# First x tiles first on the ACT ring, fold copies by PSUM bank, last tile in column halves, a new order table

## The chip, the cores and the metric

The kernel runs on one core of a Trainium2 chip. The metric is the device time of one execution in microseconds; 264.27 us is the median of four runs of the kernel before (263.08 to 264.51).

A core has five engines that run their own instruction queues in order: TensorE (PE in the profile, with its weight loads as PEld), VectorE (DVE), ScalarE (ACT), GpSimd (POOL) and SyncE (SP), which here only issues DMAs. ScalarE issues a few DMAs too. [...]

## The reference

One block with adaptive normalisation. x is [1, 2048, 448], c is [1, 448]. Six rows of modulation come from c; then a linear attention with a softmax feature map, then a gated MLP that mixes over the sequence:

```
sa, ca, ga, sb, cb, gb = silu(c) @ w_mod
h = layernorm(x) * (1 + ca) + sa
q, k, v = h @ wqkv                               # 16 heads of 28
phi(p) = concat(softmax(p @ w_phi), softmax(-p @ w_phi))
kv = phi(k)^T v ; z = sum over s of phi(k)
x = x + ga * ((phi(q) kv) / (phi(q) z + 1e-6)) @ wo
h = layernorm(x) * (1 + cb) + sb
z1, z2 = split(gelu(h @ w_in))                   # 896 columns each
g = w_sp @ layernorm(z2) + b_sp                  # w_sp is 2048 x 2048
x = x + gb * (z1 * g) @ w_out
```

All inputs and the output are bf16.

## The kernel before

The program has a fast path, and a general path behind a branch that is taken only when a bound on the exponents fails. All of the profile is the fast path. It works on 16 tiles of 128 rows of x; x stays in SBUF from the start to the end (f_x), and so do the weights. Four stages follow each other, and overlap:

* **The head**, to about 12 us. The loads are issued, x tiles 0 and 1 are normalised and transposed by TensorE (turn_mm, turn_out), the columns 1 + ca and sa are made from c and w_mod (columns, 16 tiny matmuls for each), and w_phi and 1 + ca are folded into the key weights: wk is transposed (fold_T), copied out of PSUM (L742), multiplied with a block diagonal BD of w_phi (fold_pf), and scaled (fold_W). Row 448 of the folded weights carries the bias from sa (fold_sa and the copy after it). keep_busy issues matmuls whose result nobody reads.
* **Keys and values**, to about 57 us. For each tile i: k.i and v.i are four matmuls each, e.i.0 and e.i.1 the exponentials of +p and -p, rd, rc and mu the sum, the reciprocal and the product that make the softmax, vc the copy of v, and kv eight matmuls that accumulate kv over all tiles. In between, the query weights are folded (fq, sq, pq), the second norm's columns are made (cfb), the gates (gt), and queries are projected (qp, and q for single pieces) with their exponentials (qpe, qe). gs, gr and grc square the folded weights and sum them for the bound. bn, ag, rp, la1, ld1 and lT normalise x tiles 2 to 15 and transpose them, mostly by a DMA (lT) that SP issues; tm and to do it with TensorE.
* **Outputs of the attention and the MLP's first half**, to about 137 us. For each tile: num (eight matmuls), sx, cr, dn, ri, w and t (the division and the product), ad on GpSimd, oT (a transposing DMA), wo, xc (the residual), ls, la, rs and ap (the second norm), h2T (a transposing DMA), z2 and its gelu ge, zs, za and zn (the norm of z2). z1.st.fc with its gelu zg makes z1 for four tiles at a time. ws scales the MLP's weights by 1 + cb, wg the output weights by ga.
* **The gated product**, from 137 us: for each of four column blocks of w_sp and each of seven feature blocks 16 matmuls (g_unit), then VectorE adds and multiplies, and the output tiles (o_mm, o_fin) follow one block behind.

What each engine does in which order is written by hand. The head stands as straight code; from there a string ORDER lists words like `k.3` or `e.3.0`, and a loop calls the step of each word in turn. Every step puts its instructions at the ends of its engines' queues, so the string fixes the order of each queue. `ld.n` are loads on SP's queue: 3 is x tiles 12 to 15, 4 the second 960 columns of modulation (840 KB), 7 and 9 the gates' weights, 5 and 6 the halves of w_in, 8 wo. `wsp.0.u` is one of eight transposing loads of the first w_sp block. ca and cc are memsets and small copies on GpSimd.

PSUM tiles of one bank come from four buffers (bank, bank_bf), those of two banks from two (bank2). A step that takes a buffer waits for the last reader of its former tile; most waits of TensorE on ScalarE are of this kind.

SP's and ACT's DMAs share eight completion semaphores in turn, so each DMA also waits for the one eight places ahead of it.

Of the kernel before, what the change touches and what calls it, by code (L numbers as in the profile page):

```python
# [15 lines left out]
P = 128  # L16
D = 448
# [5 lines left out]
FC = 7  # L23
# [455 lines left out]
CB = HP * DH  # L479
# [39 lines left out]


def fast_path(tc, A_x, A_wqkv, A_w_phi, A_wo, B_w_in, B_w_sp, B_b_sp, B_w_out, c, w_mod, out, flag):
# [182 lines left out]
    def l1_ag(i):  # L704
        nc.vector.bn_aggr(out=l1_pair(i), in_=l1bn.pop(i)[:])
# [7 lines left out]
    def l1_rstd(q):  # L713
        l1rs[q] = rstd_of(l1mv.pop(q), 2, "l1", RD if 2 * q in BY_ACT else -1.0)
# [67 lines left out]
    for i in range(2):  # L782
# [39 lines left out]


    Eq = eqp.tile([P, 4, 2, S], BF, name="f_Eq")
# [440 lines left out]
    nc.scalar.copy(out=ot[:, 0:D // 2], in_=last[3][:, 0:D // 2])  # L1265
    nc.scalar.dma_start(out=outv[15][:, 0:D // 2], in_=ot[:, 0:D // 2])
    nc.vector.tensor_copy(out=ot[:, D // 2:D], in_=last[3][:, D // 2:D])
# [53 lines left out]
```

## Time and profile before

| what | value |
|---|---|
| median of the runs | 264.27 us |
| profiled execution | 263.18 us |
| its span | 261.4 us |
| granted clock of TensorE | 0.994 |
| busy: PE, PEld | 248.6, 128.7 us |
| busy: DVE, ACT, POOL | 162.6, 107.8, 90.3 us |
| share of PE in the chain that ended last | 83% |
| first statistics of x (VectorE) | 5.42 us |
| first exponential of k (ScalarE) | 16.53 us |
| first num (TensorE) | 56.31 us |
| first g matmul (TensorE) | 137.28 us |

The span runs from the first to the last instruction; the execution's own time is a little longer. A matmul's end is modelled: two that follow each other overlap in the record, and the distance between starts is what one costs (four k matmuls start within 0.76 us, though they are recorded as 0.92 busy). L and a number is a line of the kernel. "issue" in the chain is time in which the engine waited for nothing that the profile shows, SPq and ACTq are the engines' queues.

### The profile page before, as it was taken

The page shows a single profiled execution, that of the slowest core. Times are in us where ns is not written, and L with a number is a line of the kernel's source. Part 1 is how long each engine was busy: PE and PEld are TensorE (multiplying, and loading weights), DVE is VectorE, ACT ScalarE, POOL GpSimd, SP SyncE. Part 2 cuts the span into 40 slices and gives each one's busy share as a digit, 9 for nine tenths or more (in the row PEclk, how much of TensorE's full clock was granted, in tenths as well). Part 3 has the DMA queues.
Part 4 walks back from the last instruction along what each step waited for, and adds up shares of the span by engine and source line. Part 5 has one row for each costly group of instructions (what it writes and reads, how often), then busy time and mean ns, then how long its engine had stood idle before and what let it go on. Part 6 is the DMA issues. An engine that isn't in the chain of part 4 may idle for free.

```text
span 261.4 us, 4412 instructions
## 1 busy us (share of the span) xinstructions
PE 248.6 (95%) x1570; PEld 128.7 (49%) x1590; DVE 162.6 (62%) x364; ACT 107.8 (41%) x208; POOL 90.3 (35%) x201
## 2 busy tenths in 40 slices
PE   6789999999998999999999999999999999999991
PEld 3555666675554555444444444444444444444450
DVE  3889989999999989968062454342533434342540
ACT  2499777979775478887986000000000000000000
POOL 5787871004888778766340092000000000000000
PEclk9999999999999999999999999999999999999997
DMA  7975889605666334144499999951000000001002
GB/s 179 294 208 100 158 174 127 214 3 42 136 119 89 63 61 63 31 91 82 83 189 191 245 185 173 171 117 36 18 0 18 20 30 5 0 20 35 19 20 63
DMA packets 69057, 25.29 MB, mean 97 GB/s; under 512 B 59105, under 2 KB 68898, under 8 KB 69026
## 3 DMA queue, kind: packets, MB, share of 16 engines
q1 hardware_dynamic: 68066, 24.12, 48.0%
q10 hardware_dynamic: 960, 0.80, 1.2%
q8 instruction: 14, 0.23, 0.4%
q14 instruction: 17, 0.14, 0.2%
HBM read 8.92 MB, written 1.84 MB: 41 GB/s over the span
## 4 chain that ended last, share of the span: by engine, by line
PE 83%; DVE 5%; DMA 4%; ACT 3%; issue 2%; POOL 1%; ACTq 0%
PE g_ps L1213 37%; PE z_ps L832 17%; PE o_ps L1220 8%; PE v_ps L832 4%; PE k_ps L832 4%; PE x_ps L1105 3%; PE kvacc L866 3%; DMA f_wm<-in_w_mod_dram 2%; PE q_ps L832 2%; DVE t L1074 2%; DMA oT<-f_opad 2%; PE num L1045 2%; PE b_ps L778 1%; ACT f_Wsq L955 1%; ACT f_E L839 0%
## 5 line engine op out<-in xcount | busy, mean ns | idle before, releaser
L1213 PE MATMUL g_ps<-f_wsp,f_z2n 128*128 128x512 bf16 x328 | 73.7, 379 | 0.4
L1213 PEld LDWEIGHTS <-f_z2n 128*128 128x128 bf16 x448 | 43.7, 98 | 52.0
L1215 DVE TENSOR_TENSOR gb<-g_ps,f_bsp 128x512 f32<-128x512 f32 x28 | 19.4, 692 | 68.1 <-PE g_ps L1213 63.6
L1265 ACT CAST ot<-o_ps 128x224 bf16<-128x224 f32 x1 | 0.3, 345 | 114.6 <-PE o_ps L1220 114.6
L832 PE MATMUL z_ps<-f_win,h2T 128*128 128x448 bf16 (+1 forms) x128 | 26.9, 352 | 0.5 <-DMA h2T<-f_xpad 0.4
L1128 DVE BATCH_NORM_STATS2 z2st<-z2g 128x6 f32<-128x448 bf16 x32 | 19.2, 614 | 11.7 <-ACT z2g L1167 11.6
L832 PE MATMUL z_ps<-h2T,f_win 128*128 128x512 bf16 (+1 forms) x107 | 26.0, 379 | 0.3
L1080 POOL TENSOR_TENSOR f_opad<-t 128x448 bf16<-128x448 bf16 x16 | 16.8, 1056 | 23.5 <-DVE t L1074 22.9
L1213 PE MATMUL g_ps<-f_hT,f_z2n 128*128 128x512 bf16 x109 | 24.7, 379 | 0.2
L1220 PE MATMUL o_ps<-f_wout,f_z1T 128*128 128x448 bf16 x112 | 23.5, 352 | 0.0
L1216 DVE TENSOR_TENSOR f_z1T<-gb,f_z1T 128x512 bf16<-128x512 f32 x28 | 20.1, 716 | 1.0
L1178 ACT ACTIVATE f_z1T<-z_ps,f_b 128x512 bf16<-128x512 f32 x28 | 18.2, 683 | 3.7 <-PE z_ps L832 3.7
L832 PEld LDWEIGHTS <-h2T 128*128 128x128 bf16 (+1 forms) x128 | 12.0, 97 | 12.0 <-DMA h2T<-f_xpad 1.0
L850 DVE TENSOR_REDUCE ksum<-f_E 128x32 f32<-128x896 bf16 x16 | 16.9, 1074 | 1.7 <-ACT f_E L839 1.5
L1171 ACT ACTIVATE f_z2n<-z2g,nm,rs 128x896 bf16<-128x896 bf16 x16 | 17.8, 1128 | 0.3 <-POOL nm L1142 0.3
L1167 ACT ACTIVATE z2g<-z_ps 128x896 bf16<-128x896 f32 x16 | 14.6, 918 | 6.7 <-PE z_ps L832 5.3
L832 PEld LDWEIGHTS <-f_win 128*128 128x128 bf16 x112 | 10.9, 97 | 12.8
L1074 DVE TENSOR_TENSOR t<-num,w 128x896 bf16<-128x896 f32 x16 | 17.0, 1085 | 0.1
L839 ACT ACTIVATE f_E<-k_ps 128x448 bf16<-128x448 f32 x32 | 16.1, 561 | 1.8 <-issue 1.1
L1220 PEld LDWEIGHTS <-f_z1T 128*128 128x128 bf16 x112 | 10.9, 98 | 10.9
L832 PEld LDWEIGHTS <-f_hT 128*128 128x128 bf16 (+1 forms) x128 | 11.5, 97 | 8.7 <-issue 0.5
L832 PE MATMUL v_ps<-f_Wv,f_hT 128*128 128x448 bf16 x64 | 14.6, 352 | 0.4 <-ACT junk L968 0.4
(148 smaller groups left out, 337.3 us busy)
## 6 DMA issues: line engine op xcount, KB each, us to landing
out_dram<-ot SPq DMA_DIRECT2D x15, 112.0 KB, 1.7
f_x<-in_A_x_dram SPq DMA_DIRECT2D x3, 448.0 KB, 6.9
f_win<-in_B_w_in_dram SPq DMA_DIRECT2D x2, 672.0 KB, 5.3
f_wm<-in_w_mod_dram SPq DMA_DIRECT2D x1, 840.0 KB, 6.8
f_wout<-in_B_w_out_dram SPq DMA_DIRECT2D x1, 784.0 KB, 5.2
f_bsp<-in_B_b_sp_dram SPq DMA_DIRECT2D x1, 512.0 KB, 5.1
f_wm<-in_w_mod_dram ACTq DMA_DIRECT2D x1, 448.0 KB, 6.3
f_wm<-in_w_mod_dram SPq DMA_DIRECT2D x1, 392.0 KB, 6.8
```

The costliest lines, as they stand in the source:

```text
L832: nc.tensor.matmul(out, lhsT=lhs(kc, last[kc]), rhs=rhs(kc, last[kc]), start=(kc == 0), stop=(kc == KC - 1))
L839: nc.scalar.activation(out=Ering[i % NR][:, s, :], in_=ps["k", i][:, 0:D], func=ACT.Exp, scale=1.0 - 2.0 * s)
L850: nc.vector.tensor_reduce(out=cs["s", i][:], in_=Ering[i % NR][:].rearrange("p s (c f h) -> p (s c) h f", c=4, h=HP), axis=AX.X, op=ALU.add)
L1074: nc.vector.tensor_tensor(out=ts[i][:, 0:2 * D].rearrange("p (s h d) -> p s h d", s=2, h=H), in0=nv(i)[:, :, :, 0:DH], in1=cs.pop(("w", i) ...
L1080: nc.gpsimd.tensor_tensor(out=opad[i % NO][:, 0:D], in0=t[:, 0:D], in1=t[:, D:2 * D], op=ALU.add)
L1128: nc.vector.bn_stats(out=cs["z", i][:, hf, :], in_=z2gs[i][:, hf * D:(hf + 1) * D])
L1171: nc.scalar.activation(out=z2n[:, i, :], in_=z2gs.pop(i)[:], func=ACT.Identity, scale=rstd[:, 1:2], bias=nmr[:, 1:2])
L1178: nc.scalar.activation(out=z1T[:, fc, st * 512:(st + 1) * 512], in_=ps.pop(("z1", st, fc)), func=ACT.Gelu_apprx_tanh, bias=b1[:, fc:fc + 1])
L1213: nc.tensor.matmul(g[:], lhsT=z2n[:, s_, fc * P:(fc + 1) * P], rhs=wsp_tiles[tcn][:, s_, :], start=(s_ == 0), stop=(s_ == NT - 1))
L1215: nc.vector.tensor_tensor(out=gb[:], in0=g[:], in1=bsp[:, tsl], op=ALU.add)
L1216: nc.vector.tensor_tensor(out=z1T[:, fc, tsl], in0=gb[:], in1=z1T[:, fc, tsl], op=ALU.mult)
L1220: nc.tensor.matmul(o_ps, lhsT=z1T[:, fc, t * P:(t + 1) * P], rhs=wout_s[:, fc, :], start=(first and fc == 0), stop=(fc == FC - 1))
```

## The change

Six things differ.

1. The load of wk's last 64 rows goes from ACT's queue to SP's, so that x tiles 0 and 1 stand first on ACT's.
2. The four copies after fold_T are given to ScalarE and VectorE by PSUM bank (g // 2) and no longer in turn (g % 2).
3. rstd of the first tiles stands before BD on GpSimd.
4. The transposes of tile 1 stand before the fold on TensorE, one keep_busy after it, and the copy of that tile goes from VectorE to ScalarE. Statistics of tile 3 stand before the order table.
5. The last output tile is made in two halves of 224 columns, each in a bank of its own, with its own copy and its own DMA.
6. ORDER is a new string with the same words except bn.3 and ag.3 (now ahead of it).

```diff
-    nc.scalar.dma_start(out=wk_raw[0:64, 3, 0:D], in_=A_wqkv[3 * P:D, D:2 * D])
-    nc.sync.dma_start(out=wk_raw[:, 0:3, 0:D], in_=A_wqkv[0:3 * P, D:2 * D].rearrange("(k p) n -> p k n", p=P))
+    load_rows(nc.sync, wk_raw[:, :, 0:D], A_wqkv[:, D:2 * D])
     nc.scalar.dma_start(out=x_sb[:, 0:2, :], in_=xv[:, 0:2, :])
...
-            (nc.vector.tensor_copy if g % 2 else nc.scalar.copy)(out=wT[:, g, 0:D], in_=tps[g // 2][0:CB, g % 2, 0:D])
+            (nc.vector.tensor_copy if g // 2 else nc.scalar.copy)(out=wT[:, g, 0:D], in_=tps[g // 2][0:CB, g % 2, 0:D])
...
+    l1_rstd(0)
     nc.gpsimd.tensor_tensor(out=BD[:].rearrange("p g (f h) -> p g f h", h=HP),
...
-    l1_rstd(0)
     more_constants()
...
     turn_out(0, hT[:, :, 0:P], True)
-    keep_busy(1, 256)
+    turn_mm(1)
     pf01 = bank2("pf01")
...
-    turn_mm(1)
+    keep_busy(1, 256)
     sa_ps = bank("sa_ps")
     fold_sa(wk_raw, sa_ps)
+    turn_out(1, hT[:, :, P:2 * P], True)
     nc.scalar.copy(out=wTk[:, :, D], in_=sa_ps[0:CB, 0:4])
     fold_pf(wTk, 3)
-    turn_out(1, hT[:, :, P:2 * P], False)
+    for i in (2, 3):
+        l1_bn(i)
+        l1_ag(i)
     fold_W(Wk, 3, True)
-    l1_bn(2)
-    l1_ag(2)
...
-    last = [bank2("o_ps")[:, 0, 0:D] if n < 2 else bank("o_ps")[:, 0:D] for n in range(4)]
+    last = [bank2("o_ps")[:, 0, 0:D] if n < 2 else bank("o_ps")[:, 0:D if n == 2 else D // 2] for n in range(5)]
...
-    nc.tensor.matmul(last[3], lhsT=ident[:], rhs=x_sb[:, 15, :], start=True, stop=False)
-    o_mm(last[3], 15, 0, 7, first=False)
     ot = wk.tile([P, D], BF, tag="ot", bufs=4)
-    nc.scalar.copy(out=ot[:, 0:D // 2], in_=last[3][:, 0:D // 2])
-    nc.scalar.dma_start(out=outv[15][:, 0:D // 2], in_=ot[:, 0:D // 2])
-    nc.vector.tensor_copy(out=ot[:, D // 2:D], in_=last[3][:, D // 2:D])
-    nc.sync.dma_start(out=outv[15][:, D // 2:D], in_=ot[:, D // 2:D])
+    for n, (eng, copy) in enumerate(((nc.scalar, nc.scalar.copy), (nc.sync, nc.vector.tensor_copy))):
+        cols = slice(n * D // 2, (n + 1) * D // 2)
+        o_ps = last[3 + n]
+        nc.tensor.matmul(o_ps, lhsT=ident[:], rhs=x_sb[:, 15, cols], start=True, stop=False)
+        for fc in range(FC):
+            nc.tensor.matmul(o_ps, lhsT=z1T[:, fc, 15 * P:16 * P], rhs=wout_s[:, fc, cols], start=False, stop=(fc == FC - 1))
+        copy(out=ot[:, cols], in_=o_ps)
+        eng.dma_start(out=outv[15][:, cols], in_=ot[:, cols])
```

Of the order table, the start, the place where the attention's outputs begin, and the end:

```diff
-cc gs.0 k.0 bv bn.3 wv.2 ag.3 wv.1 bn.4 rp.1 gr.0 bn.5 bvc k.1 ld.7 wv.0 ag.4 wv.3 ag.5 ld.3 bn.7 grc.0 sq rp.2 e.0.0 bn.6 v.0 e.1.0 ld1.3 sqc ag.7
-e.1.1 ld1.2 tm.3 ag.6 bn.10 e.0.1 fq.0 la1.5 vc.0 to.3 fq.1 ag.10 rd.0 la1.4 fqc.2 lT.5 tm.2 k.3 fqc.0 rp.3 fqc.1 to.2 gt.0 rc.0 lT.4 fqc.3 bn.8 e.3.0
...
+ca wv.3 rp.1 k.1 bv wv.0 wv.2 wv.1 bn.4 k.0 bvc bn.5 e.1.1 cc ag.4 ld.4 ld1.2 e.1.0 sq ag.5 bn.7 e.0.0 v.0 ld1.3 sqc ld.7 e.0.1 ag.7 bn.6 tm.2 tm.3
+vc.0 v.1 rp.2 to.2 gs.0 rd.0 k.2 to.3 v.2 rc.0 la1.5 bn.8 vc.1 v.3 bn.10 la1.4 vc.2 ag.6 e.2.0 fq.1 mu.0 rp.3 lT.4 e.2.1 fq.0 bn.9 vc.3 kv.0 ag.8 rd.1
...
-vc.14 zb mu.15 vc.15 wg.2 gs.1 wg.0 kv.14 wg.1 wg.3 kv.15 wb.3 kb1 wb.2 wbc.3 kb2 gr.1 wbc.2 ws.1 num.0 zbc num.1 ws.3 sx.0 q.5 sx.1 cr.0 cr.1 dn.0
...
+rc.15 kv.13 mu.15 v.15 wg.1 wg.2 kv.14 wg.0 vc.15 wb.3 qpe.1.0 kv.15 wb.2 qpe.1.1 kb2 kb1 zb wbc.3 wg.3 gr.1 ws.2 num.0 num.1 ws.1 sx.0 q.7 zbc sx.1
...
-z2.14 zg.2.2 zg.2.3 wsp.0.4 zg.2.4 z1.3.4 ge.13 z1.3.5 wsp.0.7 ge.14 z1.3.6 zs.14.0 z2.15 zg.3.6 zs.14.1 zg.3.4 za.14 zs.13.0 rs.17 z1.3.1 ge.15
-zs.13.1 z1.3.3 za.13 zg.3.1 rs.16 zs.15.0 z1.3.2 zs.15.1 zg.3.3 zn.14 z1.3.0 za.15 rs.18 zg.3.2 zn.13 zn.15 zg.3.5 zg.3.0
...
+z2.14 wsp.0.5 z1.3.6 ge.14 z1.3.3 wsp.0.2 zg.3.6 zs.14.0 zn.12 z2.15 zs.14.1 wsp.0.0 za.14 zs.13.1 zg.3.3 rs.17 z1.3.1 za.13 ge.15 z1.3.5 rs.16 zg.3.1
+zs.15.0 z1.3.0 zs.15.1 zg.3.5 z1.3.4 za.15 zg.3.0 rs.18 zn.14 z1.3.2 zn.13 zn.15 zg.2.6 zg.3.2 zg.3.4
```

Other moves in the table: ld.4 from the place after e.4.1 to the start, ahead of ld.7; ld.3 from the start to the place after gtc.0; q.11 from the attention's outputs to the keys and values; wsp.0.2 and wsp.0.5 from the attention's outputs to the end, wsp.0.4 and wsp.0.7 from the end to the keys and values; ws.2 takes the place of ws.3 ahead of the first product.

## The prediction

> **What bounds the kernel now.** I read the engines by stage first, since a mean over the span mixes stages with different limits. The table of windows gives, by stage, length, then busy time of PE, PEld, DVE, ACT and POOL:
>
> ```profile
> 0.00:12.00 12.00, 8.38 (x108) 5.63 (x109) 6.55 (x22) 4.08 (x9) 7.99 (x51) 1.00 0.90 232
> 12.00:18.00 6.00, 5.05 (x56) 2.71 (x55) 4.87 (x17) 5.69 (x13) 4.27 (x11) 1.00 0.94 261
> 18.00:57.00 39.00, 38.84 (x396) 25.16 (x398) 37.19 (x73) 31.97 (x66) 17.70 (x32) 1.00 0.69 133
> 57.00:86.00 29.00, 27.43 (x196) 15.14 (x195) 28.47 (x82) 20.61 (x55) 19.86 (x32) 1.00 0.56 88
> 86.00:137.00 51.00, 50.73 (x275) 25.24 (x278) 37.34 (x99) 40.89 (x61) 31.88 (x70) 1.00 0.46 83
> 137.00:256.00 119.00, 118.14 (x554) 54.85 (x562) 47.82 (x73) 4.43 (x7) 8.64 (x9) 1.00 0.39 74
> ```
>
> From 18 to 57 and from 86 to 256 us TensorE never rests, so the matmuls themselves set the end there. Time can only come from three places: before 18 us, the 57 to 86 us stage where VectorE is the busier engine (28.5 of 29.0), and the tail. Next the chain that ended last (start, length, what), at the head and the tail:
>
> ```profile
> 1.95 6.26 DMA f_wm<-in_w_mod_dram
> ...
> 12.77 1.31 ACT f_Wsq L955
> 14.08 0.47 ACT f_Wsq L956
> 14.55 0.56 ACT f_Wv L878
> ...
> 16.63 0.87 ACT f_E L839 x2
> 17.57 0.44 ACT f_E L839
> 18.05 1.05 PE tps L887 x16
> ...
> 255.80 0.35 ACT ot L1265
> 256.17 0.39 DVE ot L1267
> ```
>
> Between 12 and 18 us the chain is ScalarE's: the squares (word gs.0, 1.87 us) stand before the scaling of Wv and the first exponentials, and banks come free only with those. At the end two copies stand one behind the other. Third, who waited for whom (total, times, longest):
>
> ```profile
> DVE l1st L702 <- DMA f_x<-in_A_x_dram: 3.6, 1, 3.6
> PEld L770 <- DMA f_wm<-in_w_mod_dram: 1.7, 1, 1.7
> PEld L1105 <- DMA oT<-f_opad: 1.4, 3, 1.0
> DVE ot L1267 <- ACT ot L1265: 1.3, 1, 1.3
> PE num L1045 <- DVE t L1074: 0.4, 1, 0.4
> ```
>
> VectorE's first work waits for x, TensorE's first real columns for w_mod, and VectorE's last copy for ScalarE's, though both read data that was ready at 255.8.
>
> **What the Trainium skill says.** "PSUM — Partial Sum Buffer", section "PSUM bank collisions raise a hardware error", says two engines may not touch one bank and quadrant together, reads included, so software puts a dependency between them. The wait of L1267 on L1265 is that, and ends with the first copy. "DMA: Bandwidth & Descriptors", section "Queues, rings and completion order", says each DMA engine takes turns between rings it has work for: so x on the ACT ring shares with the SP ring. The trace agrees in so far as bytes and not issue times set the head (232 and 261 GB/s in the first two rows). "SBUF — State Buffer", section "Who interferes with whom", says a VectorE instruction in a two-port mode and a GpSimd one exclude each other; the trace fits: the ws scaling took 0.69 and 0.67 us beside an idle GpSimd, 0.93 and 1.45 us beside ad.0 and ad.1.
>
> **Part 1, the head.** One DMA leaves ACT's queue (issue 0.56 us), so x[0:2] is issued at 0.73 instead of 1.32 and w_mod's first piece at 1.3 instead of 1.95. SP gains an issue of about 0.45 us; wk, phi, w_mod's second piece and x[2:4] move back by that. wk landed at 4.4; at 4.9 it still beats the warm-up matmuls, which end at 5.48, so this costs nothing; beyond 5.5 it costs one for one. 56 KB less ahead of x is at most 0.59 us (the issue) and, with rings sharing some 300 GB/s, at least 0.2; I take 0.4. VectorE then runs 0.4 earlier through statistics to the two x tiles. On GpSimd BD (0.93 us) now stands behind rstd (1.64 us): ends near 9.2 instead of 6.7, just when its reader, the fold, starts, as the second transpose now stands before it. So fold_pf starts where it did (9.4) or 0.2 earlier. The fold copies by bank (two by 0.5 on ACT, 0.69 on DVE) hide under w_mod's landing: nothing. turn_out(1) goes from DVE (0.41) to ACT (0.59), fitting in the 0.63 us in which ACT waited for fold_sa. Wk complete: 12.7 to 12.9 against 12.87.
>
> **Part 2, the order up to num.0.** ScalarE pitches, from consecutive starts in the trace: exp and copies 0.43, Wv scaling 0.55. After Wk, ScalarE now does wv.0, wv.1, bvc, ending 14.5 instead of squares first; four exponentials and sqc end at 16.3 instead of 18.4, and the squares (1.78) follow vc.0 at 16.6. TensorE: k.1, bv, k.0, sq end at 14.9 (0.76+0.76+0.38 after 12.95), v.0 15.6, two transposes 16.1, v.1 from 16.3, then k.2, v.2, v.3 to 19.4, fq.1, fq.0 to 20.3. Their waits: k.2 on to.2, 16.5 against 17.1; fq.1 on vc.1, 18.8 against 19.4; kv.0 on mu.0, 19.9 against 20.3. So no idle time worth counting after 14.9, where before it lasted until 18.05.
>
> The sum over the stage: 32 k and v by 0.76 = 24.3; 16 kv by 0.42 = 6.7; two qp of eight by 0.217 = 3.5; four of 0.76 (bv, gt.0, two wb) = 3.0; the rest (transposes 1.3, sq and two gr 1.1, pq 0.8, cfb 0.8, zb 0.7) 4.7: 42.3 us. Before: num.0 starts at 56.31, the stage at 12.04: 44.3, of which 2.0 idle. After: the same plus q.11 (0.87) = 43.2 from 12.0, with 0.5 idle: num.0 at 55.7, q.11 already done. Gain 1.5; I take 1.4 for the uncertain 0.2 of part 1.
>
> What else moves. The memset of win (1.59 us, at 38.5 before, in GpSimd's idle time) now stands before rp.1, cc (2.1) before rp.2, so la1.4 ends at 19.4 instead of 18.4; its transpose (SP busy 1.2, landing 2.5) arrives at 22.0, k.4 needs it at 23.0: hidden with 1.0 to spare. SP: the 840 KB piece (ld.4), at 23.6 before, is issued at 10.6 behind the second columns' matmuls, ahead of ld.7; at 300 GB/s the 4.6 MB asked by then land by 18.8; cfb and gt.0 need them at 21.4 and 22.2. x[12:16] (ld.3) moves from 9.7 to 23.1, past three transposes, landing near 27; bn.13 needs it at 27.7. Two w_sp pieces (SP 1.3 each) leave the 57 to 86 us stage, which frees the oT transposes.
>
> **Part 3, 57 to 86 us.** VectorE starts cr.0 at 57.0 instead of 57.31 (kb1 waits for kv.15, and ws.2 replaces ws.3), and the rest of its work is the same. TensorE's waits there are 0.58, 0.30, 0.53 and 0.71 = 2.1. Going through the new order with the t products every 1.0 us I find waits of 0.4 at num.5, 0.5 at num.8, 0.2 at z2.1, 0.5 at num.11: 1.6 to 1.8. Between a gain of 0.4 and the loss of the whole lead (rival 1); I take 0.2.
>
> **Part 4, 86 to 256 us.** z1, z2 and wo are counted the same; ScalarE was at 40.9 of 51, its gaps being waits for TensorE. Its last norm, zn.15, ends at 137.7 by the count of 3 norms after zg.3.0 (134.5); the first g group needs it at 138.6. Four w_sp pieces instead of three now follow the last h2T: see rival 1. The g stage is untouched.
>
> **Part 5, the tail.** Eight 448-column matmuls become sixteen of 224: 8 by 0.189 = 16 by 0.094, and weight loads hide, as they do under 116-column matmuls (8 in 0.42); if not, 8 extra loads by 0.098 cost 0.8 at most. VectorE's copy starts at 255.80 instead of 256.17: gain 0.37.
>
> **Sum.** 1.4 + 0.2 + 0.4 = 2.0. The profiled execution took 263.18 (span 261.4), 1.1 below the median 264.27: 261.2 for its like, and 262.3 for the median.
>
> **Rivals.** (1) The lead is absorbed. VectorE has no gap from 57 to 93 us, and enters only 0.3 earlier; if TensorE's fillers (q.11 is spent) run out, gain 0.3 + 0.4: 263.6. The same size comes if the w_sp pieces bind: the last issue at 132.1 instead of 130.7 (h2T.15 at 126.5 as before) lands at 136.4, gain 0.9 + 0.4: 263.0. For it: 28.5 of 29.0. Against: TensorE did wait 2.1 there, and work done ahead need not be done later. (2) Slower: the early 840 KB. gt.0 and everything behind it in TensorE's queue waits for ld.7, behind ld.4. Each us that ld.7 lands after 22.2 costs one; break-even is 24.2, slower by 0.5% from 25.5, which needs 1.5 MB after 13 us at 120 GB/s. At 100 it lands at 28.3: loss 6.1 - 2.0, 268.4. Against: the row to 18 us shows 261; for: 133 follows, though few transfers were asked for then. (3) A larger gain, with x and w_mod both 0.6 early and 0.4 in part 3: 2.7, 261.6.
>
> **How the numbers follow.** Under 0.5%, about 1.3 us, this kernel's measurement can't tell from no change. Forecast 0.50, larger gain 0.10, rival 1 0.25, rival 2 0.15. All but 0.05 of the first two lie below 262.95, and a little of rival 1: faster 0.57, same 0.27, slower 0.16. The range 260.9 to 264.9 holds the forecast, rivals 1 and 3 and the mild end of rival 2; of the likeliest case alone it is 261.4 to 263.2.
>
> **What would show it.** Right: first exponential near 14.5, TensorE without waits from 15 us, num.0 near 55.7, g stage near 135.4, last copy of VectorE without a wait for ScalarE. Wrong: a wait of TensorE on f_wmg or on h2T and oT that grows, num.0 not before 56.3, a gap before the first g matmul on f_wsp, or waits for a bank that the reordered copies hold.

## The result

The changed kernel takes 265.91 us as the median of 40 runs (262.62 to 268.66); the kernel before, run beside it, 263.66 us (61 runs, 262.75 to 268.23). The ratio is 1.0042, 95% interval 1.0026 to 1.0058: about 1.1 us slower. (The ratio leaves out 13 of the 40 runs of the changed kernel and 2 of the 61 before it, which took over 1.5% longer than the fastest of their kernel; by the medians of all runs the difference is 2.25 us, so 1.1 us is the low end of the loss.) The forecast was 262.3, with 264.9 as the upper end of its range. The profiled execution took 265.66 us with a span of 263.9, against 263.18 and 261.4.

The windows of the changed kernel, with the columns of the prediction's table:

```profile
0.00:12.00 12.00, 8.79 (x88) 5.77 (x89) 5.25 (x20) 3.83 (x9) 8.36 (x43) 1.00 0.93 242
12.00:18.00 6.00, 5.43 (x62) 3.35 (x62) 5.78 (x18) 5.27 (x14) 3.61 (x14) 1.00 1.09 287
18.00:57.00 39.00, 38.37 (x371) 24.09 (x371) 35.60 (x71) 33.02 (x68) 19.55 (x36) 1.00 0.67 139
57.00:86.00 29.00, 26.50 (x219) 15.17 (x218) 28.86 (x83) 18.87 (x54) 18.48 (x29) 0.98 0.34 60
86.00:137.00 51.00, 50.41 (x271) 25.21 (x275) 36.76 (x97) 39.76 (x59) 31.82 (x68) 0.98 0.38 73
```

From 12 to 18 us TensorE is busier than before (5.43 against 5.05), as the order was forecast to make it. From 57 to 86 it is less busy (26.50 against 27.43), and the granted clock is below 1.00. The chain that ended last says where both losses sit (start, length, what):

```profile
1.75 4.97 DMA f_wk_raw<-in_A_wqkv_dram
6.77 1.89 PE tps L739 x16
8.65 0.85 PE warm_ps L672 x2
...
22.86 4.04 DMA f_hT<-f_xpad
26.95 0.93 PE k_ps L832 x4
...
80.16 4.53 DMA h2T<-f_xpad
84.73 3.00 PE z_ps L832 x8
```

The head now hangs on wk, which landed at 1.75 + 4.97 = 6.72 us. The first row of the table below isn't all wk's, though: fold_T's 16 transposes also took 1.89 instead of 1.18 us (tps above), as the trace records the full clock from 9.84 us on, where before the change it is from 5.71. Later two transposed tiles that usually land 2.4 to 2.5 us after their issue took 4.04 and 4.53. The waits (total, times, longest) agree, and show that the one at the tail is gone: VectorE's last copy waits for TensorE and no longer for ScalarE.

```profile
PEld L832 <- DMA h2T<-f_xpad: 3.0, 2, 2.2
PE z_ps L832 <- DMA h2T<-f_xpad: 2.3, 2, 2.0
PEld L739 <- DMA f_wk_raw<-in_A_wqkv_dram: 2.0, 1, 2.0
DVE ot L1269 <- PE o_ps L1268: 0.9, 1, 0.9
```

Where the 2.5 us of span went, from the starts of the same steps in the two traces:

| stretch | before | after | difference |
|---|---|---|---|
| start to the first k matmul | 12.04 | 13.14 | +1.10 |
| first k to num.0 (after: q.11, 0.87, done too) | 44.27 | 44.54 | +0.27 |
| num.0 to the first g matmul | 80.97 | 83.03 | +2.06 |
| first g to the first matmul of the last tile | 116.76 | 116.75 | 0.0 |
| from there to VectorE's last copy | 2.13 | 1.74 | -0.39 |
| last copy to the end of the span | 5.23 | 4.70 | -0.53 |

The third row adds up: z2.2 waited 1.99 where before two waits in that place were 0.36 and 0.56 (+1.07); the granted clock was 0.50 behind the long wait, from 84.94 to 88.35 us, so that eight z2 matmuls took 3.00 instead of 1.68 and four of wo 1.33 instead of 0.92 (+1.73); one more wait of 0.31 came at 131.6 us; the wait at 66 us shrank by 0.16, and q.11 was already done (-0.87). The sum is +2.08. One microsecond of the windows behind the wait, with the granted clock third from the end:

```profile
86.00:87.00 1.00, 1.00 (x4) 0.45 (x3) 0.89 (x2) 0.00 (x0) 0.90 (x4) 0.50 0.34 66
```

### The profile page after: what moved, and what is told of

Same layout as the page of the kernel before. It is cut to its first block, busy times and chain, and to the rows that moved or that the text cites. A ratio compares the mean times of both kernels' runs of the same rounds, so it can differ in the third digit from the quotient of the medians.

```text
span 263.9 us, 4432 instructions
## 1 busy us (share of the span) xinstructions
PE 251.1 (95%) x1578; PEld 130.8 (50%) x1598; DVE 161.2 (61%) x363; ACT 108.4 (41%) x209; POOL 92.2 (35%) x201
## 4 chain that ended last, share of the span: by engine, by line
PE 78%; DMA 7%; DVE 6%; issue 3%; POOL 3%; ACT 1%; SPq 0%; POOLq 0%; ACTq 0%
PE g_ps L1213 36%; PE z_ps L832 15%; PE o_ps L1220 8%; DMA h2T<-f_xpad 3%; PE k_ps L832 3%; PE v_ps L832 3%; PE x_ps L1105 3%; PE kvacc L866 2%; PE q_ps L832 2%; DMA f_wk_raw<-in_A_wqkv_dram 2%; DMA f_hT<-f_xpad 2%; DVE t L1074 1%; PE num L1045 1%; POOL f_xpad L689 1%; POOL rstd L680 1%
## 5 line engine op out<-in xcount | busy, mean ns | idle before, releaser
L832 PE MATMUL z_ps<-f_win,h2T 128*128 128x448 bf16 (+1 forms) x128 | 28.3, 365 | 2.3 <-DMA h2T<-f_xpad 2.3
L1213 PE MATMUL g_ps<-f_hT,f_z2n 128*128 128x512 bf16 x109 | 24.5, 379 | 0.1
L1220 PE MATMUL o_ps<-f_wout,f_z1T 128*128 128x448 bf16 x105 | 22.0, 352 | 0.0
L1216 DVE TENSOR_TENSOR f_z1T<-gb,f_z1T 128x512 bf16<-128x512 f32 x28 | 19.4, 692 | 1.2
L839 ACT ACTIVATE f_E<-k_ps 128x448 bf16<-128x448 f32 x32 | 15.5, 548 | 2.4 <-ACT f_vaug L846 0.6
L1220 PEld LDWEIGHTS <-f_z1T 128*128 128x128 bf16 x105 | 10.3, 98 | 10.3
L832 PE MATMUL k_ps<-f_Wk,f_hT 128*128 128x448 bf16 x64 | 14.6, 352 | 0.7 <-DMA f_hT<-f_xpad 0.5
```

What stands on the lines that cost most here:

```text
L832: nc.tensor.matmul(out, lhsT=lhs(kc, last[kc]), rhs=rhs(kc, last[kc]), start=(kc == 0), stop=(kc == KC - 1))
L839: nc.scalar.activation(out=Ering[i % NR][:, s, :], in_=ps["k", i][:, 0:D], func=ACT.Exp, scale=1.0 - 2.0 * s)
L1213: nc.tensor.matmul(g[:], lhsT=z2n[:, s_, fc * P:(fc + 1) * P], rhs=wsp_tiles[tcn][:, s_, :], start=(s_ == 0), stop=(s_ == NT - 1))
L1216: nc.vector.tensor_tensor(out=z1T[:, fc, tsl], in0=gb[:], in1=z1T[:, fc, tsl], op=ALU.mult)
L1220: nc.tensor.matmul(o_ps, lhsT=z1T[:, fc, t * P:(t + 1) * P], rhs=wout_s[:, fc, :], start=(first and fc == 0), stop=(fc == FC - 1))
```

## The experiments

Three theories. **A**: the loads of the head are the cause, since wk comes late. **B**: the new order is the cause, since it leaves the tile of z2.2 late. **C** refines B: that tile was issued in time, and its landing was held up by TensorE's own instruction fetch. For C the listing of the DMA queues shows a queue of kind "instruction" (q8). The Trainium skill, "Runtime: NRT & Kernel Launch", section "Instruction fetch mechanics", says that each engine's instructions are refilled in blocks of 16 KiB, 256 instructions, by a DMA queue of its own. From 137 to 256 us TensorE runs 554 matmuls and 562 to 564 weight loads in 119 us, so 256 instructions every 27 us, and q8 moves one block of 0.02 MB every 24 to 28 us there; no other engine issues enough to need that. (A second queue of this kind, q14, moves blocks of half that size.) The page calls the cost of a fetch mostly hidden; here it is not, as the runs show. Transfers of the changed kernel from 80 to 86 us, in 40 slices of 0.15 us:

```profile
DMA  9994000007999360009999500100000000019998
GB/s 218 217 220 89 4 0 0 0 7 152 220 213 217 66 109 0 0 20 186 201 203 179 27 0 7 9 7 12 10 12 0 1 0 0 0 24 186 220 218 188
...
q8 instruction: 1, 0.02, 1.5%
```

1.5% of 16 engines for 6 us is 1.4 us of one engine. The block starts at 82.2. The tile issued at 80.16 moved from 81.35 to about 82.1, but counts as landed only at 84.69. Its packets in the trace show what was late: all 512 of its data packets had started by 82.09, and 15 of the 16 reports that its semaphore counts came by 82.57. The sixteenth came at 84.69, behind the block, whose packet ran from 82.18 to 83.63. So the tile's bytes weren't late, one engine's report of them was; of the tile behind it, the last 8 KB moved from 83.6 to 84.4, at hardly more than 10 GB/s.

### wk back on two rings

```diff
-    load_rows(nc.sync, wk_raw[:, :, 0:D], A_wqkv[:, D:2 * D])
+    nc.scalar.dma_start(out=wk_raw[0:64, 3, 0:D], in_=A_wqkv[3 * P:D, D:2 * D])
+    nc.sync.dma_start(out=wk_raw[:, 0:3, 0:D], in_=A_wqkv[0:3 * P, D:2 * D].rearrange("(k p) n -> p k n", p=P))
```

> The changed kernel with one part undone: the last 64 rows of wk go back to the head of the ACT ring and the first x tiles behind them. Theory A (the late wk is the cause): fold_T starts at 5.5 us again instead of 6.8, runs in 1.2 us instead of 1.9, the first k matmul starts at 12.0 instead of 13.1, num.0 at 56.5, and the time falls by 1.0 to 1.2 us, to the time of the kernel before. Theory B (the new order is the cause, the head is taken up by slack): the first k starts at 12.0 all the same, but the time falls by less than 0.4 us, and z2.2 still waits about 2 us for its transposed tile.

Measured: 263.43 us median, ratio to the kernel before 1.0021 (1.0006 to 1.0037). fold_T started at 5.46, but ran in 1.91 us all the same, and the first k started at 12.74, not 12.04. Both theories missed something. From the timeline (start, length, engine, line, operation, tiles), and between them three lines of the chain:

```profile
8.64 1.03 POOL L789 TENSOR_TENSOR f_BD<-f_phi,f_bmask 112x448 bf16<-112x448 bf16 x1
...
8.48 1.33 DVE f_xpad L690 x2
9.85 0.40 PE t_ps L729 x4
10.25 0.61 PE pf L755 x12
...
10.09 0.76 PE L755 MATMUL pf<-f_BD,f_wTk 112*128 112x112 bf16 x12
84.50 1.69 PE L833 MATMUL z_ps<-f_win,h2T 128*128 128x448 bf16 x8 [2.01 <-DMA h2T<-f_xpad]
```

What held pf until 10.09 is the early turn of the second tile (t_ps), which now stands ahead of it on TensorE and waited for VectorE's scaling of that tile (f_xpad) until 9.85. BD, now behind rstd, ended before that, at 9.67. It ran beside f_xpad, which took 1.33 us for the two tiles; where BD came first it took 1.00 (the kernel before) and 0.99 (the run with BD first, below). So with x no longer early, the early turn costs, and the swap on GpSimd may cost through VectorE. z2.2 waited 2.01 again, and this time the clock held (1.69).

### The kernel before, wk on one ring

The reverse of that diff, in the kernel before.

> The kernel before with the move of the transfers alone (wk whole on SP, the first x tiles first on ACT). Theory A: fold_T starts at 6.8 us, the first k at 13.1, num.0 at 57.4, the time rises by 1.0 to 1.2 us. Theory B: the same head, but the later stages take it up, and the time rises by less than 0.4 us.

Measured: 267.43 us, ratio 1.0177 (1.0158 to 1.0195): 4.7 us slower by the ratio, far more than either theory said.

```profile
8.12 1.49 PE L739 MATMUL tps<-f_ident,f_wk_raw 128*128 128x128 bf16 x16 [2.63 <-DMA f_wk_raw<-in_A_wqkv_dram]
8.49 0.93 POOL L787 TENSOR_TENSOR f_BD<-f_phi,f_bmask 112x448 bf16<-112x448 bf16 x1 [5.21 <-DMA f_phi<-in_A_w_phi_dram]
9.51 0.24 POOL L679 TENSOR_SCALAR rstd<-l1mv 128x2 f32<-128x2 f32 x1
```

Two things are late: wk, and w_phi behind it on SP, for which BD and with it rstd wait on GpSimd. The order of BD and rstd in the changed kernel lets rstd go ahead of w_phi. The move by itself is the worst part of the change. The trace is of the fastest of only five runs and accounts for 2.7 us (num.0 at 58.98 instead of 56.31), part of it under a clock of 0.50 from 8.59 to 12.00 us; the other 2 us aren't shown.

### The last tile in halves

The diff of the tail alone, in the kernel before.

> The kernel before with the last tile in two column halves alone. By the prediction's tail the last copy starts right behind the last matmul instead of 0.37 us behind the other copy: 0.4 us faster, 0.1 us more or less. Rival: the two last transfers end when they ended, since the second is issued only 0.4 us earlier and its landing sets the end: 0.0 us.

Measured: 262.26 us, ratio 0.9975 (0.9959 to 0.9992): 0.66 us faster, the expected 0.4 inside the interval. The copy of VectorE starts as the last matmul ends (254.75 + 0.83):

```profile
254.75 0.83 PE L1268 MATMUL o_ps<-f_wout,f_z1T 128*128 128x224 bf16 x7
254.90 0.34 ACT L1269 CAST ot<-o_ps 128x224 bf16<-128x224 f32 x1 [113.83 <-DMA out_dram<-ot]
255.62 0.39 DVE L1269 CAST ot<-o_ps 128x224 bf16<-128x224 f32 x1 [0.91 <-PE o_ps L1268]
```

### Twenty matmuls more in the head

```diff
+    keep_busy(20, 1)
     fold_T(wk_raw, wTk)
```

> The changed kernel with 20 one-column matmuls more (40 TensorE instructions with their loads) in the time in which fold_T waits for wk; they cost at most 0.3 us there. Theory C (the transposed tile of z2.2 came late because TensorE's own instruction fetch of about 20 KB, one for every 256 or so instructions, ran beside it): the fetch near 82 us now comes 2 to 3 us earlier against the work, the tile lands 2.4 to 2.5 us after its issue, z2.2 waits under 0.5 us, and the time falls by 1.5 us or more if the fetch meets no other tile that is waited for. Theory B (the order leaves the tile late): it is issued 2.5 us or less before z2.2 could start and z2.2 waits 1.5 us or more as before.

Measured: 265.7 us, ratio 1.0104 (1.0089 to 1.0118). The block of instructions started at 80.67 while num.0 was 0.74 later than in the changed kernel, so 2.2 us earlier against the work. z2.2 waited for nothing; the oT tile issued before its tile landed after 4.0 us, and wo waited for that:

```profile
83.44 0.93 PE L1106 MATMUL x_ps<-f_wo,oT 128*128 128x448 bf16 x4 [1.14 <-DMA oT<-f_opad]
```

The wait moved as C said, and fell from 1.99 to 1.14, but the condition of its time forecast wasn't met: another tile that is waited for took the delay. The time didn't fall: the ratio is 0.6% above the changed kernel's. The trace is of the fastest of the five runs (264.06), so it doesn't show why. In it wk landed at 7.35 and the first k started 0.17 later than in the changed kernel; most of the 0.74 at num.0 came behind that, where the clock was 0.50 from 13.11 to 16.52 us.

### The modulation weights behind wk

```diff
-    nc.scalar.dma_start(out=wm1[:, :, D:960], in_=wmod_v[:, :, D:960])
...
         nc.sync.dma_start(out=phi[:], in_=A_w_phi.rearrange("(g l) d f -> (l d) g f", l=4))
+    nc.sync.dma_start(out=wm1[:, :, D:960], in_=wmod_v[:, :, D:960])
```

> The changed kernel with the first 448 KB piece of the modulation weights taken from the ACT ring, where it is issued at 1.2 us beside wk, and issued on SP behind wk and w_phi. Theory A1 (wk is late because that piece and the x tiles take its bandwidth): wk lands by about 5.2 us, fold_T starts at 5.5, ahead of any wait, and the modulation columns become the next to wait (their piece lands at 7 us or later). Theory A2 (wk is late because it is all on one ring, behind its own small piece, and issued 0.6 us later): wk lands at 6.3 or later again, and fold_T waits 0.7 us or more. The time is not what this run is for: between 263.5 and 266.

Measured: 263.17 us (261.2 to 267.56), just under the range given for it, ratio 0.9984 (0.9958 to 1.0011): 0.58%, some 1.5 us, faster than the whole change. The large piece of wk in the listing of loads (KB, us from issue to landing), first of the kernel before, then of the changed kernel, of the kernel before with wk on one ring, and of this run:

```profile
f_wk_raw<-in_A_wqkv_dram SPq DMA_DIRECT2D x1, 336.0 KB, 3.3
```

```profile
f_wm<-in_w_mod_dram ACTq DMA_DIRECT2D x1, 448.0 KB, 4.4
f_wk_raw<-in_A_wqkv_dram SPq DMA_DIRECT2D x1, 336.0 KB, 5.0
```

```profile
f_wk_raw<-in_A_wqkv_dram SPq DMA_DIRECT2D x1, 336.0 KB, 6.3
```

```profile
f_wk_raw<-in_A_wqkv_dram SPq DMA_DIRECT2D x1, 336.0 KB, 4.2
```

With the 448 KB out of the way wk landed at 5.95 instead of 6.7 to 8.1, between A1 and A2: by these single traces competition for bandwidth explains 0.8 to 2.1 us of the delay, the later issue 0.6, and about 0.9 stays with the one ring and with x ahead. The warm-up ended late in this run (5.83), so wk cost almost nothing, and the columns became the next to wait, at 8.29 us, where they stood before the change too:

```profile
8.29 0.25 PE L769 MATMUL cf<-f_scol,f_wm 112*128 112x1 bf16 x4 [0.56 <-DMA f_wm<-in_w_mod_dram]
```

So x, though its statistics started at 3.4 us instead of 5.4, bought nothing: the first k started at 12.16, not before 12.04.

### wk on two rings, BD first

The first diff, and BD ahead of rstd again:

```diff
-    l1_rstd(0)
     nc.gpsimd.tensor_tensor(out=BD[:].rearrange("p g (f h) -> p g f h", h=HP),
...
+    l1_rstd(0)
     more_constants()
```

> The changed kernel with wk on two rings again and the BD product ahead of the row statistics on GpSimd again, as before; the copies by bank, the new order and the halved last tile stay. In the run with wk alone put back BD ended at 9.67 us and pf waited for it until 10.09. Theory A (the head alone loses, the order is even or a small gain): pf at 9.4 to 9.5, the first k at 12.1, 0.6 us less than with wk alone put back, so level with the kernel before or up to 0.4 us faster. Theory B (the new order costs by itself): first k at 12.1, but z2.2 still waits 2 us and the time stays 0.3 us or more above the kernel before.

Measured: 262.7 us, ratio 0.9984 (0.9963 to 1.0004). That is the time of theory A. Against the whole change (1.0042) the two edits are worth 0.58%, 1.5 us; BD first alone is 0.37% of it (1.0021 with wk alone put back), 1.0 us, of which the two traces show 0.22 at the first k and 0.63 at num.0. Against the halved tile alone (0.9975) the rest of the change, mainly the order, is 0.09% slower, 0.2 us, less than the intervals tell. The first k started at 12.52 (expected 12.1: that took BD for what pf waits for, but pf still stood behind the early turn and started at 9.86), and z2.2 waited as B had it:

```profile
83.81 1.95 PE L833 MATMUL z_ps<-f_win,h2T 128*128 128x448 bf16 x8 [1.93 <-DMA h2T<-f_xpad]
```

### The same with 14 and 28 instructions more

```diff
-    keep_busy(7)
+    keep_busy(14, 256)
```

and `keep_busy(21, 170)` in the second: the warm-up has the same number of columns, cut into more matmuls.

> As a_rings_bd, and the first seven 512-column warm-up matmuls cut into 14 of 256 columns: 14 TensorE instructions more, in no more time. By theory C the instruction fetch near 82 us comes about 0.7 us earlier against the work; it still overlaps the tile that z2.2 needs or the oT tile before it, so a wait of 0.5 to 2 us stays at one of the two.

> As a_rings_bd, and the warm-up cut into 21 matmuls of 170 columns: 28 TensorE instructions more, in no more time. By theory C the fetch comes 1.3 to 1.5 us earlier than in a_rings_bd: z2.2 waits under 0.5 us, and the oT tile issued before it is late instead (landing 3.5 to 4.1 us after its issue instead of 2.4), with a wait of 0.5 to 1.2 us at the wo matmul that reads it. If the waits do not move with the number of instructions, theory C is wrong.

Measured: with 14, 262.04 us, ratio 0.9948 (0.9926 to 0.9969), the fastest kernel of this study; with 28, 262.84 us, 0.9978 (0.9959 to 0.9996). Against num.0 the block came 1.4 us earlier in both (23.05 us behind it, where it was 24.5), twice the expected shift in the first and no more in the second, so the shift isn't proportional. The wait changed its place in both, from the tile of z2.2 to an oT tile, here first with 14, then with 28:

```profile
81.60 0.93 PE L1106 MATMUL x_ps<-f_wo,oT 128*128 128x448 bf16 x4 [1.46 <-DMA oT<-f_opad]
```

```profile
24.59 0.93 PE L833 MATMUL k_ps<-f_Wk,f_hT 128*128 128x448 bf16 x4 [0.84 <-DMA f_hT<-f_xpad]
82.38 0.93 PE L1106 MATMUL x_ps<-f_wo,oT 128*128 128x448 bf16 x4 [1.25 <-DMA oT<-f_opad]
```

With 28 an earlier block met a tile of the keys' stage as well (0.84 at 24.6 us). By the ratios the 14 are worth 0.95 us. The two traces differ by 2.6 us of span: the wait is 0.47 of it, the clock at 0.50 behind it for 3.41 us about 1.7 (estimated as half of that), and num.0 was 0.55 earlier, which is ahead of the block. So how much of the 0.95 is the block's doing isn't shown here.

### The kernel before with halves, and 14 instructions more

The same diff of keep_busy on the run with the halved tile: the test in which C forecasts a loss from an edit that takes no time.

> The kernel before with the halved last tile, and the first seven 512-column warm-up matmuls cut into 14 of 256 columns: 14 TensorE instructions more in no more time, and nothing else. By theory C the instruction fetch, which near 81 us met an oT tile (landing 4.1 us) with little waiting for it, comes 0.7 to 1 us earlier and meets the tile that z2.2 needs, issued at 79.4: its landing goes from 2.5 to 4 us or more, z2.2 waits 1.5 to 2 us instead of 0.33, and the kernel becomes 1.0 to 1.6 us slower than with the halved tile alone (262.3 us), that is 0.4 to 1.0 us slower than the kernel before. Rival: 14 instructions that take no time change nothing, within 0.3 us.

Measured: 263.27 us, ratio 1.0011 (0.9993 to 1.003), against 0.9975 without the 14: 0.36%, 0.95 us slower, at the lower end of what C expected. The first k started at 12.09, num.0 at 56.37 (12.14 and 56.41 without), so nothing was lost up to there. z2.2 without and with them:

```profile
81.94 1.69 PE L832 MATMUL z_ps<-f_win,h2T 128*128 128x448 bf16 x8 [0.33 <-DMA h2T<-f_xpad]
```

```profile
83.44 1.69 PE L832 MATMUL z_ps<-f_win,h2T 128*128 128x448 bf16 x8 [1.86 <-DVE num L1062]
```

The second wait is put down to VectorE, which was the last to signal by the record; the tile of z2.2, issued at 79.37, took 4.0 us to land (2.5 without), which is 83.4.

### The second tile's turn moved back

```diff
-    turn_mm(1)
+    keep_busy(1, 256)
     pf01 = bank2("pf01")
...
-    keep_busy(1, 256)
+    turn_mm(1)
     sa_ps = bank("sa_ps")
```

on the kernel with 14 instructions more.

> The best so far (wk on two rings, BD first, 14 warm-up matmuls) with the second x tile's turn on TensorE moved back behind the shift columns, where it stood before the change, and the 256-column filler ahead of pf again. If the early turn is what keeps the first k at 12.36 us instead of 12.04, pf starts at 9.3 to 9.4 instead of 9.9 and the first k at 12.0 to 12.1; the time falls by 0.2 to 0.4 us if nothing later takes it up, and not at all if the later stages wait for the row statistics instead.

Measured: the first k at 11.99 as expected, 0.37 earlier, and yet 263.37 us, ratio 1.002 (0.9998 to 1.0042), not 0.2 to 0.4 us faster but 1.9 us slower than the kernel it came from. Its trace shows a wait of 1.13 for a transposed tile at 24.5 us, and z2.2 waiting 1.32 for its own (landing 3.90): with the head moved, the blocks met other tiles. It is of the fastest of the 21 runs, though (262.55, against 261.93 for the trace it is compared with), so it shows 0.6 of the 1.9 us.

### The fold copies by bank, and the fastest again

`g // 2` for `g % 2` in fold_T, alone in the kernel before:

> The kernel before with the fold copies split by PSUM bank alone. The prediction put this at nothing, since VectorE comes to its two copies only at 7.4 us, behind the row statistics, when ScalarE's two are done: VectorE's copies end at 8.1 as before, the first k at 12.0, the time within 0.3 us of the kernel before. The number of TensorE instructions is the same, so by theory C the waits near 82 us stay as they are. Rival: ScalarE and VectorE no longer meet in one bank, the copies end earlier and the first k comes up to 0.3 us earlier.

Measured: 263.07 us, ratio 0.9998 (0.9983 to 1.0013). VectorE's copies start where ScalarE's have just ended, as before:

```profile
6.55 0.97 ACT L742 COPY f_wTk<-tps 112x448 bf16<-112x448 bf16 x2 [2.53 <-PE tps L740]
7.53 0.68 DVE L742 COPY f_wTk<-tps 112x448 bf16<-112x448 bf16 x2
```

The first k started at 12.12. This holds while wk is early: in the kernel before with wk on one ring, where the copies are still taken in turn, ScalarE's and VectorE's alternated from 8.80 to 10.62 us and VectorE's waited for ScalarE's. What the split is worth there wasn't measured.

> The fastest version so far once more, to see whether it stays ahead: by theory C which tile the fetch meets hangs on tenths of a microsecond, so the ratio to the kernel before may come out between 0.993 and 0.999, and the profile may show the wait at the oT tile (1.2 to 1.5 us) or at the tile of z2.2 (1.3 to 2.0 us). A ratio above 1.0 would say that its gain was chance.

Measured: 262.22 us, ratio 0.9944 (0.9928 to 0.9961). The gain stays, some 1.5 us against the kernel before. The wait was at the oT tile again, 1.25 us.

### All traces together

For each run, when the block near 80 us began (to 0.2 us), the transposed tile issued before it that landed late, its landing, and TensorE's wait:

| run | block | tile, issue | landing | wait |
|---|---|---|---|---|
| before | 81.6 | oT, 80.74 | 4.1 | 0.56 |
| halves | 81.8 | oT, 80.81 | 4.0 | 0.47 |
| copies by bank | 82.8 | oT, 82.05 | 4.0 | 0.43 |
| before, one ring | 84.4 | oT, 83.38 | 4.4 | 0.81 |
| halves, 14 more | 80.4 | h2T, 79.37 | 4.0 | 1.86 |
| after, 20 more | 80.6 | oT, 79.3 | 4.0 | 1.14 |
| after, w_mod behind | 81.4 | oT, 80.49 | 4.2 | 1.44 |
| after | 82.0 | h2T, 80.16 | 4.53 | 1.99 |
| two rings | 81.8 | h2T, 79.93 | 4.53 | 2.01 |
| two rings, BD first | 81.2 | h2T, 79.28 | 4.49 | 1.93 |
| the same, 14 more | 79.2 | oT, 77.2 | 4.3 | 1.46 |
| the same, 28 more | 80.2 | oT, 78.2 | 4.1 | 1.25 |
| 14 more, turn back | 80.4 | h2T, 79.59 | 3.90 | 1.32 |
| two rings, BD first, 14 more, again | 82.8 | oT, 80.82 | 4.1 | 1.25 |

In each the late tile is one whose 2.4 us of landing the block overlaps; the others of those stretches, apart from the tile just behind it, land in 2.4 to 2.5. The count over all fourteen traces says the same. It takes the 401 tiles oT and h2T whose landing is on record. 260 had no block near them, from 1.5 us before their issue to 2.15 us behind it, and landed after 2.40 to 2.62 us. 22 had a block of q8 that started 0.95 to 2.15 us behind their issue, and landed after 3.87 to 4.39. The smaller blocks of q14 count too: 25 tiles that one met 1.3 to 2.1 us behind their issue landed after 3.14 to 3.82. What is late depends on where the block stands: where it came 2.0 us behind the issue, 15 of the tile's 16 reports were in time, as shown above; where it came 1.0 us behind it, all sixteen were late. A run without these fetches wasn't tried. Each trace is of one execution, and within one kernel the runs differ by 1.5 to 6.4 us, so the waits explain these executions, and the medians only as far as others are like them.

## Why the prediction was wrong

**Part 1, the failed step.** The step that failed is "at 4.9 it still beats the warm-up matmuls, which end at 5.48, so this costs nothing": wk landed at 6.72. The step moved wk by one issue and counted the bytes ahead of x, but not those that now run beside wk: x and 448 KB of w_mod, issued 0.6 and 0.76 earlier. "Beyond 5.5 it costs one for one" came near by luck: fold_T started 1.29 later and the first k 1.10, but in between fold_T ran 0.71 longer, and 1.17 us in which TensorE had waited for w_mod before the change took up as much. The gain of x was mis-sized the other way (its statistics came 1.9 earlier, not 0.4) and was worth nothing: x's scaling stands behind VectorE's fold copies, which waited 3.04 us for wk's transposes, and with wk earlier w_mod was next. The early turn of tile 1, put at nothing, cost 0.37 at the first k, as it puts x's chain ahead of pf. BD behind rstd was harmless only while x was early. The copies by bank were nothing in the kernel before, as said.

**Part 2.** From the first k to num.0 the idle time was to fall from 2.0 to 0.5; it fell to 44.54 - 43.2 = 1.3, of which 0.52 is k.5's wait for a tile that landed in 4.04 us, with a block of instructions starting at 23.9. The mechanism was right (the first exponential came 0.8 earlier although the head was 1.1 later), the term mis-sized.

**Part 3, the second failed step.** Four small waits, 1.6 to 1.8 in all, were forecast, and none at z2.2, as no late landing was reckoned with (part 2 takes 2.5 us for one). One wait of 1.99 came instead, for a tile that landed in 4.53, and the clock was 0.50 for 3.41 us behind it.

**Parts 4 and 5.** The g stage is the same to 0.01 us. The tail's gain was forecast as 0.37 and measured as 0.39 in the trace.

**The rivals.** Rival 2, the early 840 KB, didn't happen: no wait on f_wmg shows. Rival 1 has the right sign of a lost lead, but not its cause; VectorE was not what z2.2 waited for. No rival had a late wk. Two of the signs of being wrong came true: num.0 started at 57.68, not before 56.3, and the wait on an h2T tile grew.

**The sum of the parts, by ratios.** The ring of wk and the swap on GpSimd +1.5 us (1.0042 against 0.9984), the tail -0.66, the order and the rest of the head +0.2: +1.1, as measured. The order's worth depends on the blocks: even with the old order in one alignment (0.9984 against 0.9975), and ahead by 0.6%, some 1.7 us, with 14 instructions more in both (0.9948 and 0.9944 against 1.0011).

## What to carry to other kernels

A load that is hurried takes bandwidth from those beside it: before moving one, ask which of them was last to be needed, and whether the hurried one was. Where waits for transposed tiles are tight, the fetch of an engine's own instructions is one more transfer, and its place depends on how many instructions come first; so compare two orders at more than one offset before giving the difference to the order. A few free instructions more or less are a cheap way to do so.

## What was not expected of the hardware

A block of TensorE's instructions (0.02 MB, 1.4 us of one DMA engine) that started 0.95 to 2.15 us behind the issue of a transposing DMA brought its landing from between 2.4 and 2.6 us to between 3.9 and 4.5. Fourteen instructions that take no time moved a kernel by 0.95 us. A load of 336 KB behind a 56 KB one on one ring landed 4.2 to 6.3 us after its issue, and 3.3 to 3.4 us with the small one on the other ring. fold_T's 16 transposes took between 1.18 and 1.91 us with no change to them or to the warm-up, and after a wait of 1.9 to 2.0 us TensorE's clock held in two runs (1.69 us for eight matmuls) and gave way in two others (1.95 and 3.00). The clock records of the traces explain the first. fold_T was quick where the full clock is recorded from before it (1.06 and 1.07 us, from 5.25 and 6.28) and slow where only from behind it (1.89 and 1.91, from 9.84 and 8.44).

Where the clock gave way it was 0.50 for 3.41 us, in one trace for 10.24. This happened in six of the fourteen traces, in four of them before 18 us. Counted in steps of 3.41 us from the first record, the long wait fell into one step in both traces that gave way, and left TensorE's recorded matmuls 42 and 44% of it. In one that held, the wait was split between two steps (70 and 72%); in the other it fell into one as well (46%). Two of the early ones came behind steps of 75 and 77%. So the share of one step fits the scatter, but no limit comes out of these. The Trainium skill, "TensorE: Matmul & The Clock Gate", section "What's actually happening", says that the activity which sets the clock is counted in free-running windows of some 3.4 us, so that the moment varies from run to run; the scatter and the steps of 3.41 us agree. But the six steps behind which the clock gave way had TensorE busy for 23 to 77%, where the page asks for one idle window, and what counts as idle stays open.
